# Reordering the start of an attention kernel by the parts of its loads, and moving one normalisation to DMA transposes

## The chip, the core and the metric

The kernel runs on one core of a Trainium2 chip. The metric is the device time of one execution in microseconds (us), quoted as the median of several runs. Every run quoted here is a fast one, so nothing below compares runs of different states. "Slot" and "iteration" are the kernel's own units: the attention part is a loop of 128 iterations (one key/value group and one tile of 128 query rows each), and every iteration has eight slots, each with one pair of score matmuls and one exponential over 128x1024 elements.

## The reference, cut to what matters

```python
mod = (_silu(c) @ w_mod).reshape(c.shape[0], 6, 1, -1)      # 512 -> 6 x 512
sa, ca, ga, sb, cb, gb = ...                                 # its six rows
h = _layernorm(x) * (1 + ca) + sa                            # x: 2048 x 512
x = x + ga * attention(h @ wq, k_cache, v_cache) @ wo        # 32 heads, 8 KV heads, Dh = 128
h = _layernorm(x) * (1 + cb) + sb
x = x + gb * mlp(h)                                          # gated MLP with a spatial mix
```

Before the first score can be computed, the first tile of x must be normalised, the modulation columns `ca` and `sa` must be computed from 1 MB of `w_mod`, the tile must be transposed and modulated, multiplied by 512 KB of `wq`, and the keys must be transposed. All of that happens once, in the first 12 us.

## The kernel before: the parts that the change touches

The loads at the start are all issued on the same queue, in this order:

```python
nc.sync.dma_start(out=x_sb[:, 0, :], in_=x_dram[:, 0, :])
nc.sync.dma_start(out=wmod_a[:], in_=wmod_dram[:, :, 0 : 2 * D])          # 1 MB, one load
k_nat = early.tile([P, SK], BF16, name="kT")
nc.sync.dma_start(out=k_nat[:, 0:HK].rearrange("p (t d) -> p t d", d=DH), in_=k_rows)
...
load_wq(0, nc.sync)                                                        # 512 KB
nc.sync.dma_start(out=x_sb[:, 1:CT, :], in_=x_dram[:, 1:CT, :])
```

The modulation is computed column by column, so that its first column already needs the whole of `wmod_a`. Then come the transposes of the first tile, the K transposes with one copy, and the projection:

```python
warm(14)                                     # zero matmuls that keep TensorE busy
xns0 = ln1_norm(0, 1, ln1_stats(0, 1))
mod_columns(0, wmod_a, 0)                    # for each of 8 columns: 4 matmuls, kt = 0..3
ln1_turn(0, 1, xns0, on_act=(1, 3))          # 2 x (2 transposes, 1 DVE and 1 ACT copy of one bank)
k_ps = bank("o_ps")[:].bitcast(BF16)
for kt in range(NKT // 2):                   # 8 transposes of K
    nc.tensor.transpose(k_ps[:, kt * P : (kt + 1) * P], k_nat[:, ...], ident[:])
nc.scalar.copy(out=kT0[:, 0:HK], in_=k_ps)
warm(1)
... qproj(0, list(range(REP)), 0, P, two_engines=True) ...   # 16 matmuls, DVE and ACT copy halves
warm(2)
first = dict(r1=ln1_stats(1, 1))             # statistics of tile 1 (the second tile)
ln_stats(mv1, 2, x_sb[:, 2, :])
first["x1"] = ln1_norm(1, 1, first["r1"])    # xn of the second tile
...
```

Chunk 1 (rows 512 to 1023) was normalised in iteration 1 and transposed by 16 TensorE transposes in its last slot, while chunks 2 and 3 already used DMA transposes:

```python
if ch == 1:
    at(*turn, lambda: ln1_turn(ch * CT, CT, st["x"]))
else:
    at(norm[0], norm[1] + 1, lambda: ln1_dma(ch * CT, CT, st["x"]))
    at(*turn, lambda: ln1_dma_mod(ch))

ln1_at(1, (1, 1), (1, 5), (1, 7))            # statistics, normalisation, transposes
```

## Time and profile before

| | before |
|---|---|
| time, median of 6 runs | 1326.84 us (1326.76 to 1327.12) |
| span of the profiled run | 1325.4 us |
| TensorE busy | 98% |
| ScalarE busy | 81% |
| VectorE busy | 36% |
| first scores start | 11.71 us |
| TensorE gap at chunk 1's transposes | scores reappear at 29.23 us, ScalarE idle 2.16 us |

The lines themselves stand in the prediction below. In a line of the timeline the columns are: start in us, length in us, engine, source line, operation, output<-input, shape, and how many instructions the line sums up. What stands in brackets at the end is the idle time of that engine before the line, and the instruction that ended it. Source lines differ between the kernels, because the change adds lines: the scores are L928 before and L980 after, the exponentials L935 and L987, the projection of the first tile L885 and L921, the copies of q L897/L899 and L929.

### The profile page before, as it was taken

To read this page: it belongs to the slowest core of one execution; us is meant where nothing else is said; L and a number is where in the kernel's file an instruction comes from. 1 tells how busy PE (TensorE), PEld (TensorE's weight loads), DVE (VectorE), ACT (ScalarE), POOL (GpSimd) and SP (SyncE) were. 2 spreads that over 40 slices of the span, in tenths; PEclk is the share of its full clock that TensorE was granted. 3 is DMA by queue.
4 is the path that set the end of the run, shared out by engine and by line. 5 is a ranking of instruction groups with operands and counts; after the bars stand their busy time and mean duration, and the time that the engine had idled before them with its cause. 6 is when DMAs were issued, how large, how long until landed. Compare 5 with 4: busy or idle time off the path is not lost.

```text
span 1325.4 us, 27685 instructions
## 1 busy us (share of the span) xinstructions
PE 1302.4 (98%) x12142; PEld 859.2 (65%) x12349; DVE 473.3 (36%) x1166; ACT 1078.4 (81%) x1061; POOL 49.0 (4%) x92
## 2 busy tenths in 40 slices
PE   8999999999999999999999999999999999999997
PEld 5666666666666666666666666666666666644444
DVE  5532222222222222222222222222222566793444
ACT  6898999999999999999999999999999999650000
POOL 1200000000000000000000000000000000120000
PEclk9999999999999999999999999999999999999999
DMA  5451021102111111111110211021101121143300
GB/s 162 111 134 30 16 49 37 37 13 53 23 31 33 34 37 37 29 37 37 33 33 17 53 37 31 19 52 25 30 13 21 25 34 33 29 115 82 66 21 27
DMA packets 145984, 57.59 MB, mean 43 GB/s; under 512 B 136160, under 2 KB 141408, under 8 KB 145856
## 3 DMA queue, kind: packets, MB, share of 16 engines
q1 hardware_dynamic: 139200, 37.32, 14.4%
q0 software_dynamic: 4208, 16.39, 4.4%
q10 hardware_dynamic: 2448, 2.03, 0.6%
q8 instruction: 98, 1.61, 0.5%
q14 instruction: 30, 0.25, 0.1%
HBM read 21.37 MB, written 2.10 MB: 18 GB/s over the span
## 4 chain that ended last, share of the span: by engine, by line
PE 97%; issue 1%; DVE 1%; DMA 0%; POOL 0%; ACT 0%; SPq 0%; DVEq 0%
PE s_ps L928 35%; PE o_ps L950 35%; PE misc L885 7%; PE misc L1290 7%; PE misc L982 6%; PE s_ps L1136 2%; PE s_ps L1175 2%; PE o_ps L1311 1%; DMA wmod_a<-in_w_mod_dram 0%; PE s_ps L1311 0%; DVE bnst L691 0%; PE misc L833 0%; DVE xn L680 0%; PE misc L782 0%; PE misc L1052 0%
## 5 line engine op out<-in xcount | busy, mean ns | idle before, releaser
L935 ACT ACTIVATE pT<-s_ps 128x1024 bf16<-128x1024 f32 x1024 | 1044.5, 1024 | 84.3 <-PE s_ps L928 10.1
L950 PEld LDWEIGHTS <-pT 128*128 128x128 bf16 x8192 | 548.5, 98 | 241.2
L950 PE MATMUL o_ps<-v,pT 128*128 128x129 bf16 x8192 | 631.4, 220 | 0.0
L928 PE MATMUL s_ps<-qT,kT 128*128 128x512 bf16 x2048 | 609.0, 379 | 10.3 <-ACT qT L899 0.5
L961 DVE RECIPROCAL rall<-o_ps 128x2 f32<-128x2 f32 x256 | 43.7, 171 | 743.6 <-PE o_ps L950 743.3
L928 PEld LDWEIGHTS <-kT 128*128 128x128 bf16 x2048 | 199.2, 98 | 119.5 <-issue 1.2
L885 PE MATMUL misc<-hT,wq_g 128*128 128x512 bf16 (+2 forms) x482 | 167.8, 365 | 0.3 <-ACT hT L842 0.2
L982 PE MATMUL misc<-wo_g,oT 128*128 128x512 bf16 x385 | 145.9, 379 | 0.0
L962 DVE TENSOR_TENSOR onorm<-o_ps,rall 128x256 bf16<-128x256 f32 x256 | 108.7, 425 | 8.8
L1290 PE MATMUL misc<-wsp,z 128*128 128x512 bf16 (+2 forms) x555 | 100.5, 336 | 0.6 <-issue 0.3
L897 DVE CAST qT<-misc 128x512 bf16<-128x512 f32 (+1 forms) x128 | 86.9, 679 | 7.6 <-PE misc L885 7.5
L1290 PEld LDWEIGHTS <-z 128*128 128x128 bf16 x560 | 50.6, 98 | 48.5
L995 DVE TENSOR_TENSOR xacc<-misc,xacc 128x512 f32<-128x512 f32 x112 | 76.2, 680 | 0.0
L885 PEld LDWEIGHTS <-wq_g 128*128 128x128 bf16 x544 | 51.5, 98 | 1.5 <-DMA wq_g<-in_A_wq_dram 0.3
L982 PEld LDWEIGHTS <-oT 128*128 128x128 bf16 x512 | 50.1, 98 | 0.7
L1305 DVE TENSOR_TENSOR gb<-misc,bsp_bc 128x512 bf16<-128x512 f32 (+1 forms) x28 | 18.4, 658 | 58.3 <-PE misc L1290 58.3
L1136 PE MATMUL s_ps<-win_sb,hT 128*128 128x448 bf16 x128 | 27.0, 352 | 0.1
L1146 ACT ACTIVATE z<-s_ps 128x896 bf16<-128x896 f32 x16 | 14.7, 917 | 14.9 <-PE s_ps L1136 14.9
L1175 PE MATMUL s_ps<-hT,win_sb 128*128 128x512 bf16 x109 | 24.3, 379 | 0.2
L1183 ACT ACTIVATE z1T<-s_ps 128x1024 bf16<-128x1024 f32 x14 | 14.3, 1024 | 10.1 <-PE s_ps L1175 9.1
L691 DVE BATCH_NORM_STATS2 bnst<-x_sb 128x6 f32<-128x512 bf16 x32 | 21.8, 682 | 0.5
L706 POOL DMA_DIRECT2D wq_g<-in_A_wq_dram x7 | 5.3, 753 | 420.9 <-PE misc L885 420.9
(79 smaller groups left out, 279.5 us busy)
## 6 DMA issues: line engine op xcount, KB each, us to landing
wq_g<-in_A_wq_dram POOLq DMA_DIRECT2D x7, 512.0 KB, 3.9
v<-in_A_v_cache_dram POOLq DMA_DIRECT2D x7, 512.0 KB, 6.6
wo_g<-in_A_wo_dram POOLq DMA_DIRECT2D x7, 512.0 KB, 4.7
oT<-onorm SPq DMA_TRANSPOSE x128, 2.4
wsp<-in_w_mod_dram POOLq DMA_DIRECT2D x1, 2048.0 KB, 9.1
out_dram<-yout ACTq DMA_DIRECT2D x15, 128.0 KB, 1.7
win_sb<-in_B_w_in_dram POOLq DMA_DIRECT2D x1, 1792.0 KB, 9.4
x_sb<-in_A_x_dram SPq DMA_DIRECT2D x3, 512.0 KB, 5.5
```

What stands on the lines that cost most here:

```text
L885: nc.tensor.matmul(ps[0][:, o0 : o0 + n], lhsT=wqs[g][:, dt, hh * DH : (hh + 1) * DH], rhs=hTs[ch][:, dt, c0 : c0 + n], start=(dt == 0), s ...
L897: nc.vector.tensor_copy(out=dst[:, 0:cut], in_=src[:, 0:cut])
L928: nc.tensor.matmul(s_ps[:, h * 512 : (h + 1) * 512].rearrange("p (r q) -> p r q", r=REP), lhsT=groups[g]["kT"][:, kt * P : (kt + 1) * P], ...
L935: nc.scalar.activation(out=pTs[u][:, 2 * i : 2 * i + 2, :], in_=s_ps[:].rearrange("p (k q) -> p k q", k=2), func=ACT.Exp, scale=inv_sqrt_dh,)
L950: nc.tensor.matmul(o_ps[:, hh % 2, 0 : DH + 1], lhsT=pTs[u][:, kt, hh * P : (hh + 1) * P], rhs=groups[g]["v1"][:, kt, 0 : DH + 1], start=( ...
L961: nc.vector.reciprocal(out=rall[:, c0 : c0 + 2], in_=o_ps[:, :, DH])
L962: nc.vector.tensor_tensor(out=onorms[u][:, hh - 1 : hh + 1, :], in0=o_ps[:, :, 0:DH], in1=rall[:, c0 : c0 + 2].unsqueeze(2).to_broadcast([ ...
L982: nc.tensor.matmul(X_ps[:], lhsT=oTs[u][:, hh, :], rhs=groups[g]["wo"][:, hh, :], start=(hh == 0), stop=(hh == REP - 1),)
L995: nc.vector.tensor_tensor(out=xaccs[j][:], in0=X_ps[:], in1=xaccs[j][:], op=ALU.add)
L1136: nc.tensor.matmul(ps[0][:, hf * 512 : hf * 512 + FC], lhsT=h2Ts[j // CT][:, dt, (j % CT) * P : (j % CT + 1) * P], rhs=win_sb[:, dt, FH + ...
L1175: nc.tensor.matmul(ps[0][:, k * 512 : (k + 1) * 512], lhsT=win_sb[:, dt, f * P : (f + 1) * P], rhs=h2Ts[2 * ch2 + k][:, dt, :], start=(dt ...
L1290: nc.tensor.matmul(g_ps[:, :n], lhsT=z2[:, st, f * P : (f + 1) * P], rhs=wsp[t][:, st, c0 : c0 + n], start=(st == 0), stop=(st == NT - 1 a ...
```

## The change

The intent is that work on the first tile starts when a part of a load is there, not the whole, and that DVE and ACT never copy out of the same PSUM bank. On top of this, chunk 1 takes the DMA path that chunks 2 and 3 already have. The parts are: (1) `wmod` in four loads and the modulation summed part by part; (2) half of K loaded behind `wq`; (3) the first tile's transposes on two banks, and its projection into a tile of two banks; (4) the second K half copied by DVE behind the first scores, ahead of the second tile's normalisation; (5) chunk 1 by DMA transposes, with its statistics two slots earlier and its projection four slots later.

```diff
-    nc.sync.dma_start(out=wmod_a[:], in_=wmod_dram[:, :, 0 : 2 * D])
+    for kt in range(NDT):
+        nc.sync.dma_start(out=wmod_a[:, kt, :], in_=wmod_dram[:, kt, 0 : 2 * D])
...  (k_nat is loaded in two halves; the second one behind wq)
     load_wq(0, nc.sync)
+    load_k_nat(1)
     nc.sync.dma_start(out=x_sb[:, 1:CT, :], in_=x_dram[:, 1:CT, :])
...
-    warm(14)
     xns0 = ln1_norm(0, 1, ln1_stats(0, 1))
-    mod_columns(0, wmod_a, 0)
-    ln1_turn(0, 1, xns0, on_act=(1, 3))
...
+    mc_ps = bank("misc")
+    warm(10)
+    for kt in range(NDT - 1):
+        mod_part(kt, mc_ps)            # 8 one-column matmuls on part kt
+        warm(2)
+    ...                                # 4 transposes of xn, two in each of two banks
+    mod_part(NDT - 1, mc_ps)
+    mod_copy(0, mc_ps)
+    ...                                # hT: DVE copies one bank, ACT the other
+    k_turn((0, 1, 2, 3), (nc.vector.tensor_copy, nc.scalar.copy))
+    qTs = {0: early.tile([P, REP, 512], BF16, name="qT")}
+    q_ps = bank2()                     # ONE tile of two banks
+    ...                                # 16 projection matmuls, heads 0-1 in bank 0, 2-3 in bank 1
+    for hf, copy in enumerate((nc.vector.tensor_copy, nc.scalar.copy)):
+        copy(
+            out=qTs[0][:, 2 * hf : 2 * hf + 2, 0:P],
+            in_=q_ps[:, hf * 512 : hf * 512 + 2 * P].rearrange("p (h q) -> p h q", h=2),
+        )
...
+    def first_norm():                  # placed behind the first scores
+        k_turn((4, 5, 6, 7), (nc.vector.tensor_copy,))
+        ln_stats(mv1, 2, x_sb[:, 2, :])
+        first["x1"] = ln1_norm(1, 1, first["r1"])
...
-    ln1_at(1, (1, 1), (1, 5), (1, 7))
+    ln1_at(1, (0, 7), (1, 2), (2, 2))
...
-                it, slot = 2 + (2 + k) // 16, (1 + k // 2) % 8
+                it, slot = 2 + (10 + k) // 16, (5 + k // 2) % 8
```

More of the change, by code (lines that the diff above doesn't have):

```diff
@@ L697, with load_k_nat @@
     nc.sync.dma_start(out=x_sb[:, 0, :], in_=x_dram[:, 0, :])
-    nc.sync.dma_start(out=wmod_a[:], in_=wmod_dram[:, :, 0 : 2 * D])
+    for kt in range(NDT):
+        nc.sync.dma_start(out=wmod_a[:, kt, :], in_=wmod_dram[:, kt, 0 : 2 * D])
     k_nat = early.tile([P, SK], BF16, name="kT")
-    nc.sync.dma_start(out=k_nat[:, 0:HK].rearrange("p (t d) -> p t d", d=DH), in_=k_rows)
-    groups, wqs, hTs, qTs = {}, {}, {}, {}
+    def load_k_nat(half):
+        t0, t1 = half * NKT // 4, (half + 1) * NKT // 4
+        nc.sync.dma_start(
+            out=k_nat[:, t0 * P : t1 * P].rearrange("p (t d) -> p t d", d=DH),
+            in_=k_rows[:, t0:t1, :],
+        )
+    load_k_nat(0)
+    groups, wqs, hTs = {}, {}, {}
     def load_wq(g, engine):
@@ L788, in mod_columns, with mod_copy @@
                     )
+        mod_copy(first, mc_ps)
+    def mod_copy(first, mc_ps):
         c0 = first * NDT
@@ L822, in ln1_mod, with ln1_turn @@
         )
-    def ln1_turn(j0, n, xns, on_act=()):
+    def ln1_turn(j0, n, xns):
         ch, c0 = j0 // CT, (j0 % CT) * P
@@ L840, in ln1_turn @@
                 dst, src = hT[:, dt, c0 : c0 + n * P], t_ps[:, k, 0 : n * P]
-                if dt in on_act:
-                    nc.scalar.activation(
-                        out=dst,
-                        in_=src,
-                        func=ACT.Identity,
-                        scale=modc[:, NDT + dt : NDT + dt + 1],
-                        bias=modc[:, dt : dt + 1],
-                    )
-                else:
-                    ln1_mod(dst, src, dt)
+                ln1_mod(dst, src, dt)
     def ln1_dma(j0, n, xns):
@@ L859, in ln1_dma_mod, with mod_part @@
             ln1_mod(hTs[ch][:, dt, :], hTs[ch][:, dt, :], dt)
-    warm(14)
-    xns0 = ln1_norm(0, 1, ln1_stats(0, 1))
-    mod_columns(0, wmod_a, 0)
-    ln1_turn(0, 1, xns0, on_act=(1, 3))
-    k_ps = bank("o_ps")[:].bitcast(BF16)
-    for kt in range(NKT // 2):
-        nc.tensor.transpose(
-            k_ps[:, kt * P : (kt + 1) * P], k_nat[:, kt * P : (kt + 1) * P], ident[:]
-        )
-    nc.scalar.copy(out=kT0[:, 0:HK], in_=k_ps)
+    def mod_part(kt, mc_ps):
+        for col in range(2 * NDT):
+            nc.tensor.matmul(
+                mc_ps[:, col : col + 1],
+                lhsT=wmod_a[:, kt, col * P : (col + 1) * P],
+                rhs=sc_bf[:, kt : kt + 1],
+                start=(kt == 0 and col == 0),
+                stop=(kt == NDT - 1 and col == 2 * NDT - 1),
+            )
@@ new lines, in k_turn @@
+    def k_turn(kts, copies):
+        n = len(kts) // len(copies)
+        for e, copy in enumerate(copies):
+            part = kts[e * n : (e + 1) * n]
+            k_ps = bank("o_ps")[:].bitcast(BF16)
+            for k, kt in enumerate(part):
+                nc.tensor.transpose(
+                    k_ps[:, k * P : (k + 1) * P], k_nat[:, kt * P : (kt + 1) * P], ident[:]
+                )
+            copy(out=kT0[:, part[0] * P : (part[-1] + 1) * P], in_=k_ps[:, 0 : n * P])
+    xns0 = ln1_norm(0, 1, ln1_stats(0, 1))
@@ new lines @@
+    mc_ps = bank("misc")
[3 more added lines that the diff above has]
+        warm(2)
+    x_ps = []
+    for half in range(2):
+        x_ps.append(bank(("misc", "o_ps")[half])[:].bitcast(BF16))
+        for k in range(2):
+            dt = 2 * half + k
+            nc.tensor.transpose(
+                x_ps[half][:, k * P : (k + 1) * P], xns0[0][:, dt * P : (dt + 1) * P], ident[:]
+            )
+    mod_part(NDT - 1, mc_ps)
+    mod_copy(0, mc_ps)
+    hT_of(0)
@@ new lines @@
+    for k in range(2):
+        ln1_mod(hTs[0][:, k, 0:P], x_ps[0][:, k * P : (k + 1) * P], k)
+        nc.scalar.activation(
+            out=hTs[0][:, 2 + k, 0:P],
+            in_=x_ps[1][:, k * P : (k + 1) * P],
+            func=ACT.Identity,
+            scale=modc[:, NDT + 2 + k : NDT + 3 + k],
+            bias=modc[:, 2 + k : 3 + k],
+        )
+    k_turn((0, 1, 2, 3), (nc.vector.tensor_copy, nc.scalar.copy))
+    qTs = {0: early.tile([P, REP, 512], BF16, name="qT")}
+    q_ps = bank2()
@@ new lines @@
+    for n, dt in enumerate((0, 2, 1, 3)):
+        for hh in range(REP):
+            c0 = hh // 2 * 512 + hh % 2 * P
+            nc.tensor.matmul(
+                q_ps[:, c0 : c0 + P],
+                lhsT=wqs[0][:, dt, hh * DH : (hh + 1) * DH],
+                rhs=hTs[0][:, dt, 0:P],
+                start=(n == 0 and hh % 2 == 0),
+                stop=(n == NDT - 1 and hh % 2 == 1),
+            )
+    for hf, copy in enumerate((nc.vector.tensor_copy, nc.scalar.copy)):
+        copy(
+            out=qTs[0][:, 2 * hf : 2 * hf + 2, 0:P],
+            in_=q_ps[:, hf * 512 : hf * 512 + 2 * P].rearrange("p (h q) -> p h q", h=2),
+        )
@@ L871, with qproj @@
     warm(1)
-    def qproj(b, heads, c0, n, two_engines=False):
+    def qproj(b, heads, c0, n):
         g, ch = divmod(b, NCH)
@@ L895, in mm @@
                 src = ps[0][:, 0 : len(hs) * n].rearrange("p (h q) -> p h q", q=n)
-                cut = len(hs) // 2 if two_engines else len(hs)
-                nc.vector.tensor_copy(out=dst[:, 0:cut], in_=src[:, 0:cut])
-                if two_engines:
-                    nc.scalar.copy(out=dst[:, cut:], in_=src[:, cut:])
+                nc.vector.tensor_copy(out=dst, in_=src)
         return [lambda hh=hh, dt=dt: mm(hh, dt) for hh in heads for dt in range(NDT)]
-    for fn in qproj(0, list(range(REP)), 0, P, two_engines=True):
-        fn()
-    warm(2)
     first = dict(r1=ln1_stats(1, 1))
-    ln_stats(mv1, 2, x_sb[:, 2, :])
-    first["x1"] = ln1_norm(1, 1, first["r1"])
-    ln_stats(mv1, 3, x_sb[:, 3, :])
-    first["r2"] = rstd_of(mv1[:, 2:4, :], 2, "ln1")
     NU = HKV * NT
@@ L1069 @@
     fill = {}
+    def first_norm():
+        k_turn((4, 5, 6, 7), (nc.vector.tensor_copy,))
+        ln_stats(mv1, 2, x_sb[:, 2, :])
+        first["x1"] = ln1_norm(1, 1, first["r1"])
+        ln_stats(mv1, 3, x_sb[:, 3, :])
+        first["r2"] = rstd_of(mv1[:, 2:4, :], 2, "ln1")
     def first_turn():
@@ L1075 @@
     at(0, 5, lambda: ln1_turn(2, 2, first["x2"]))
-    for i in (0, 1, 2, 4):
+    fill[0, 0] = [first_norm]
+    for i in (1, 2, 4):
         fill[0, i] = [lambda: warm(1)]
@@ L1085, in ln1_at @@
         at(*norm, lambda: st.update(x=ln1_norm(ch * CT, CT, st["r"])))
-        if ch == 1:
-            at(*turn, lambda: ln1_turn(ch * CT, CT, st["x"]))
-        else:
-            at(norm[0], norm[1] + 1, lambda: ln1_dma(ch * CT, CT, st["x"]))
-            at(*turn, lambda: ln1_dma_mod(ch))
-    ln1_at(1, (1, 1), (1, 5), (1, 7))
+        at(norm[0], norm[1] + 1, lambda: ln1_dma(ch * CT, CT, st["x"]))
+        at(*turn, lambda: ln1_dma_mod(ch))
+    ln1_at(1, (0, 7), (1, 2), (2, 2))
     ln1_at(2, (2, 4), (3, 1), (4, 5))
```

## The prediction

> **What bounds the kernel now.** I read the page of the profile first: busy time by engine and the chain that ended last.
>
> ```profile
> PE 1302.4 (98%) x12142; PEld 859.2 (65%) x12349; DVE 473.3 (36%) x1166; ACT 1078.4 (81%) x1061; POOL 49.0 (4%) x92
> ...
> PE 97%; issue 1%; DVE 1%; DMA 0%; POOL 0%; ACT 0%; SPq 0%; DVEq 0%
> ```
>
> TensorE is busy 98% of a span of 1325.4 us and makes up 97% of the chain. No later wait is long enough to swallow a saving, so whatever TensorE gains near the start should reach the end. All TensorE idleness together is 1325.4 - 1302.4 = 23 us, and warm-up matmuls count as busy, so this change of the first 50 us can win a few microseconds, never the 26.5 us that would be 2%.
>
> Then I read the timeline of the first 50 us. The start:
>
> ```profile
> 5.88 0.41 DVE L680 TENSOR_SCALAR xn<-x_sb,mv,rstd_ln 128x512 bf16<-128x512 bf16 x1 [1.02 <-POOL rstd_ln L676]
> ...
> 7.34 0.95 PE L782 MATMUL misc<-sc_bf,wmod_a 128*128 128x1 bf16 x32 [1.30 <-DMA wmod_a<-in_w_mod_dram]
> ...
> 8.41 0.15 DVE L791 TENSOR_SCALAR modc<-misc 128x4 f32<-128x4 f32 x1
> ...
> 9.05 0.81 ACT L842 ACTIVATE hT<-misc,modc 128x128 bf16<-128x128 bf16 x2 [5.82 <-DVE hT L815]
> ...
> 9.54 1.08 PEld L885 LDWEIGHTS <-wq_g 128*128 128x128 bf16 x16 [0.30 <-DMA wq_g<-in_A_wq_dram]
> ...
> 10.83 0.42 DVE L897 CAST qT<-misc 128x256 bf16<-128x256 f32 x1 [1.54 <-PE misc L885]
> ...
> 11.17 0.68 DVE L691 BATCH_NORM_STATS2 bnst<-x_sb 128x6 f32<-128x512 bf16 x1
> 11.29 0.37 ACT L899 CAST qT<-misc 128x256 bf16<-128x256 f32 x1 [0.53 <-DVE qT L897]
> 11.71 0.59 PE L928 MATMUL s_ps<-qT,kT 128*128 128x512 bf16 x2 [0.49 <-ACT qT L899]
> ```
>
> Two loads (wmod, then wq) and two serial pairs of copies decide when the first scores (L928) start, at 11.71. The second query tile then waits for its own normalisation; here are its xn, its transposes, and the scores behind them:
>
> ```profile
> 13.09 0.41 DVE L680 TENSOR_SCALAR xn<-x_sb,mv,rstd_ln 128x512 bf16<-128x512 bf16 x1 [0.22 <-POOL rstd_ln L676]
> ...
> 13.56 0.40 PE L833 MATMUL misc<-ident,xn 128*128 128x128 bf16 x4 [0.39 <-DVE xn L680]
> ...
> 13.79 0.59 PE L928 MATMUL s_ps<-qT,kT 128*128 128x512 bf16 x2
> ```
>
> And the one large hole afterwards, the normalisation of chunk 1:
>
> ```profile
> 26.36 0.61 PE L950 MATMUL o_ps<-v,pT 128*128 128x129 bf16 x8
> ...
> 27.53 1.87 PE L833 MATMUL misc<-ident,xn 128*128 128x128 bf16 x16 [0.56 <-DVE xn L680]
> ...
> 29.23 0.59 PE L928 MATMUL s_ps<-qT,kT 128*128 128x512 bf16 x2
> ...
> 29.86 2.89 ACT L935 ACTIVATE pT<-s_ps 128x1024 bf16<-128x1024 f32 x3 [2.16 <-PE s_ps L928]
> ```
>
> The in-order TensorE reaches 16 transposes whose input the DVE and GpSimd have not finished. The last of the eight o_ps matmuls has issued by 26.36 + 0.61 - 0.22 (one matmul's latency) + 0.06 = 26.80; the next scores start at 29.23. ScalarE starves for 2.16 us.
>
> [...] ACT's hT at 9.05 waits for DVE's hT, ACT's CAST of qT at 11.29 waits 0.53 us for DVE's CAST, both pairs from one bank. [...] So the single 1 MB wmod load releases nothing before its end (issue to landing 6.1 us here), and four loads give four release points. [...] (0.95 - 0.16)/31 = 25 ns for the one-column matmuls, 0.59 - 0.38 = 0.21 us for scores. [...] Here a 128x512 bf16 scaling from PSUM takes 0.54 us (0.45 apart), from SBUF 0.41 us (0.33 apart).
>
> **Part 1, wmod in four loads, modulation by part.** Same bytes, same 2 KB pieces, same queue: the last part should land where the whole did, about 7.3. Three quarters of the 32 one-column matmuls and the four transposes of xn (ready at 6.3) move ahead of that. After the landing there remain 8 matmuls: 24 x 25 ns = 0.6 us saved, so the modc copies start near 7.7 instead of 8.33. With x_ps on two banks, DVE does two hT copies and ACT two, side by side: about 8.1 to 8.7 and 8.1 to 8.9, where ACT ended at 9.86 before.
>
> **Part 2, half of K after wq.** hT is now ready before wq, so wq's landing binds: 2.57 + 6.9 = 9.47 before. 128 KB fewer are ahead of it; at the roughly 380 GB/s that the queue moved in that stretch this is 0.34 us, so about 9.15. I assume the extra issues on SP (about 0.4 us each) stay hidden behind the backlog of the queue.
>
> **Part 3, projection.** 16 matmuls x 56 ns + 0.22 = 1.1 us, so 10.3; the two qT copies now read two banks in parallel: 0.42 instead of 11.66 - 10.83 = 0.83. First scores at 10.3 + 0.42 + 0.05 = 10.8, that is 0.9 earlier.
>
> **Part 4, the second tile gives most of that back.** The second K half is copied by the DVE behind the first scores, in front of the second tile's xn. First statistics: x_sb tiles 1 to 3 land at 3.04 + 7.5 = 10.54, so 10.65. K copy after the K transposes: 10.8 + 0.43 (two scores issued) + 0.44 (four transposes with latency) = 11.65, for 0.5. Statistics of tile 2 from 12.1, aggregation 12.8, xn at 12.9 instead of 13.09. TensorE then idles between the second scores and the transposes, as before. So from the third slot on the shift is only 0.2 us.
>
> **Part 5, chunk 1 by DMA transposes.** Sixteen TensorE transposes (0.9 us) and the wait before them go. Scores could start at 26.80 instead of 29.23, a gain of 2.43. But ScalarE is the pacer just there: with two score buffers, scores of a slot wait for the exp two slots back. Its run of six from 22.10 lasts 5.60, to 27.70; so iteration 2 starts at 27.75 instead of 30.12: 2.36. The five slots of iteration 2 without projection then run at ScalarE's 0.905 instead of TensorE's 0.885: minus 0.1. What replaces it: statistics (4 x 0.79 on DVE) from about 18.3, xn by 24.4, four DMA transposes (1.2 us of SP each, 2.5 to land) by about 30, modulation about 31.4, first projection with it about 32.5. It should not wait. Moving the projection from slots 1 to 7 of iteration 2 into iterations 2 and 3 leaves its sum alone.
>
> **Sum.** 2.36 - 0.1 + 0.2 = about 2.5 us. 1326.8 - 2.5 = 1324.3 us.
>
> **The rivals.** (a) The new chunk 1 path is late: the DMA transposes land after 32.5, and TensorE waits at the first projection of chunk 1. For it: later ones of this kind took 3.6 to 14.7 us to land; against: those ran beside a 2 MB load, and at 25 to 30 us the queues are empty. It would cost 1 to 2 us: 1325.5. (b) SP becomes the limit at the start: eight issues before the x tiles instead of five; if they stall, wq and the x tiles land up to 1 us later and the K copy in front of xn makes the second tile later than before. For it: one earlier issue took 1.35 us, the transposing one 3.3 us. It would turn the +0.2 into -0.6: 1325.1. (c) The early start carries through, because the x tiles come sooner or the DVE order costs less: up to 0.9 more, 1323.5. (d) Nothing arrives, ScalarE taking over as bound: against it, ACT is at 81% and shows 0.2 to 0.3 us of idleness per slot with projection.
>
> **Range and chances.** Centre 1324.3; (a) and (b) set the upper edge at 1325.7, (c) the lower one at 1323.0. 2% either way lies ten times outside these terms: faster 0.005, within 2% 0.99, slower 0.005.
>
> **What would show it.** Right: first scores near 10.8, modc near 7.7, no L885 wait but for wq; xn of tile 2 near 12.9; no hole of TensorE near 27; iteration 2's first scores near 27.6; 17 TensorE matmuls fewer. Wrong: TensorE idle before the first projection of chunk 1 near 32 (rival a), wq landing at or after 9.5 (b), or ScalarE without gaps through iterations 2 and 3 (d).

In the paragraph ahead of Part 1 are readings of the trace of before. The 56 ns of Part 3 are in that trace, too: (0.61 - 0.22)/7 from its eight K transposes (L867, 0.61 us together, 219 ns for one). What rested on the cut passages was the author's estimate: that copies out of two banks run side by side, and that a load releases nothing before its end. For the second, the traces have this: with one load, landed at 7.30 (1.19 + 6.11), the first modulation matmul started at 7.34; with four, in the changed kernel, the parts ran at 4.94, 5.88, 6.52 and 7.39.

## The result and the profile after

The changed kernel takes 1325.82 us (median of 6 runs, 1325.43 to 1326.52) against 1326.84 us (6 runs, 1326.76 to 1327.12). Ratios here are the mean time of one kernel's fast runs over that of the other's fast runs of the same rounds, so they are not quite the ratio of the medians quoted: 0.9993, with a 95% interval of 0.998 to 1.0006. The interval includes 1, though the slowest run of the changed kernel (1326.52) is below the fastest of before (1326.76). That is "the same" at 2%, and a gain of 1.0 us in the medians. The prediction was 1324.3 with a range up to 1325.7: it claimed 2.5 us and 1.0 us came. Note also the spread: 1.1 us between the changed kernel's runs, 0.4 us before.

First the page of the changed kernel: busy time by engine, and the chain that ended last.

```profile
PE 1313.2 (99%) x12332; PEld 858.6 (65%) x12332; DVE 473.2 (36%) x1168; ACT 1077.8 (81%) x1061; POOL 49.4 (4%) x92
...
PE 98%; DMA 0%; DVE 0%; SPq 0%; issue 0%; ACT 0%
```

The bound has not changed. The TensorE figures of the two pages can't be compared by themselves, because the trace of before lacks about 200 matmul records (12142, against 12349 weight loads). The weight loads can: 12349 before, 12332 now, 17 fewer, as predicted.

Next the timeline of the start of the changed kernel, in the order of the prediction's steps.

```profile
7.77 0.16 DVE L803 COPY modc<-misc 128x4 f32<-128x4 f32 x1 [1.48 <-PE misc L868]
...
8.10 0.81 ACT L908 ACTIVATE hT<-o_ps,modc 128x128 bf16<-128x128 bf16 x2 [4.87 <-DVE modc L804]
...
9.63 0.90 PEld L921 LDWEIGHTS <-wq_g 128*128 128x128 bf16 x16 [0.57 <-DMA wq_g<-in_A_wq_dram]
...
10.74 0.42 DVE L929 CAST qT<-s_ps 128x256 bf16<-128x256 f32 x1 [1.91 <-PE s_ps L921]
...
11.20 0.37 ACT L929 CAST qT<-s_ps 128x256 bf16<-128x256 f32 x1 [1.56 <-DVE qT L929]
11.62 1.01 PE L980 MATMUL s_ps<-qT,kT 128*128 128x512 bf16 x2 [0.70 <-ACT qT L929]
...
13.09 0.42 DVE L886 COPY kT<-o_ps 128x512 bf16<-128x512 bf16 x1 [1.11 <-PE o_ps L883]
13.44 0.69 DVE L691 BATCH_NORM_STATS2 bnst<-x_sb 128x6 f32<-128x512 bf16 x1
...
14.25 0.38 DVE L680 TENSOR_SCALAR xn<-x_sb,mv,rstd_ln 128x512 bf16<-128x512 bf16 x1
```

Three things are to be seen. The modulation and hT come when they were expected (7.77 and 8.10), in this profile; the experiments show (end of e11) that this was the earliest of six. TensorE then waits for `wq` until 9.63, later than before (9.54). And ACT's copy of q at 11.20 still waits for DVE's copy. So the first scores start at 11.62, only 0.09 us earlier than before. Everything behind them is later: xn of the second tile comes at 14.25, where it was 13.09.

Part of this lateness has a cause that the prediction did not name. The first scores took 1.01 us where a pair took 0.59 before. The view by stretches of time gives, for each stretch, its length, then busy time and instructions of PE, PEld, DVE, ACT and POOL, then the granted TensorE clock, DMA share and GB/s. The stretch from 11 to 14 us of the changed kernel:

```profile
11.00:14.00 3.00, 2.38 (x9) 0.97 (x8) 1.85 (x5) 1.45 (x3) 0.81 (x2) 0.55 1.31 246
```

The granted clock is 0.55 there. The clock records of the trace put the half clock at 11.27 to 14.68 us, 3.41 us long. No such stretch is in the profile of before at this place.

The second half of the story is chunk 1. The view by stretches for 26 to 31 us, before and then after:

```profile
26.00:31.00 5.00, 4.17 (x48) 2.88 (x46) 3.44 (x11) 2.84 (x4) 1.02 (x1) 1.00 0.02 5
```

```profile
26.00:31.00 5.00, 5.00 (x58) 3.69 (x56) 0.86 (x3) 5.00 (x7) 0.00 (x0) 1.00 0.65 107
```

The hole is gone: TensorE and ScalarE are busy for all of the 5 us, where ScalarE was busy for 2.84. The timeline shows that nothing takes its place when the transposed chunk is first used:

```profile
23.23 12.02 ACT L987 ACTIVATE pT<-s_ps 128x1024 bf16<-128x1024 f32 x13 [0.41 <-PE s_ps L980]
...
24.79 5.18 SPq L859 DMA_TRANSPOSE hT<-xn  x4
...
32.49 1.38 DVE L828 TENSOR_SCALAR hT<-hT,modc 128x512 bf16<-128x512 bf16 x4 [2.81 <-DMA hT<-xn]
...
34.35 0.59 PE L947 MATMUL misc<-hT,wq_g 128*128 128x512 bf16 x2
```

Thirteen exponentials run without a gap from 23.23 to 35.25. The DMA transposes landed about 2.4 us later than the prediction's "about 30", yet the modulation is over at 33.87 and the projection follows at 34.35 directly behind other TensorE work.

To see where time comes and goes, compare the start of every exponential with the same one before. Minus is earlier than before:

```
                       iteration,slot   0,0    0,1    0,2    1,6    1,7    2,5    from 3,5 on
changed, profiled run                  +0.32  +0.68  +1.13  +1.13  -1.19  -2.79   -1.07
```

The start loses 1.13 us, chunk 1 gains 2.32 us (from +1.13 to -1.19), and moving the projection from iteration 2 into iteration 3 gives and takes back the same amount but 0.12. From there the shift is constant until the end of attention.

### The profile page after: what moved, and what is told of

Its sections match the earlier page's. It is cut to its first block, busy times and chain, and to the rows that moved or that the text cites. A ratio compares the mean times of both kernels' runs of the same rounds, so it can differ in the third digit from the quotient of the medians.

```text
span 1324.6 us, 27877 instructions
## 1 busy us (share of the span) xinstructions
PE 1313.2 (99%) x12332; PEld 858.6 (65%) x12332; DVE 473.2 (36%) x1168; ACT 1077.8 (81%) x1061; POOL 49.4 (4%) x92
## 4 chain that ended last, share of the span: by engine, by line
PE 98%; DMA 0%; DVE 0%; SPq 0%; issue 0%; ACT 0%
PE o_ps L1002 35%; PE s_ps L980 33%; PE misc L1034 8%; PE misc L947 8%; PE misc L1347 7%; PE s_ps L1193 2%; PE s_ps L1232 2%; PE o_ps L1368 1%; PE s_ps L1368 1%; DMA wq_g<-in_A_wq_dram 0%; PE misc L1104 0%; SPq L699 0%; PE misc L1355 0%; PE s_ps L921 0%; PE misc L846 0%; DVE yout L1384 0%
## 5 line engine op out<-in xcount | busy, mean ns | idle before, releaser
L1034 PE MATMUL misc<-wo_g,oT 128*128 128x512 bf16 x512 | 194.0, 379 | 0.0
L947 PE MATMUL misc<-hT,wq_g 128*128 128x512 bf16 (+2 forms) x528 | 189.6, 371 | 0.0
L958 DVE CAST qT<-misc 128x512 bf16<-128x512 f32 x127 | 86.3, 680 | 2.0 <-PE misc L947 1.9
```

The costliest lines, as they stand in the source:

```text
L947: nc.tensor.matmul(ps[0][:, o0 : o0 + n], lhsT=wqs[g][:, dt, hh * DH : (hh + 1) * DH], rhs=hTs[ch][:, dt, c0 : c0 + n], start=(dt == 0), s ...
L958: nc.vector.tensor_copy(out=dst, in_=src)
L1034: nc.tensor.matmul(X_ps[:], lhsT=oTs[u][:, hh, :], rhs=groups[g]["wo"][:, hh, :], start=(hh == 0), stop=(hh == REP - 1),)
```

## The experiments

All twelve gave correct results, and all are "the same" at the 2% level; what is read here are tenths. The sets ran on different chips (e1 to e4 on one, e0 and e5 to e7 on a second, e8 to e10 on a third, e11 on a fourth). The 95% interval of the ratio leaves out 1 for e1 (0.9965 to 0.9998), e10 (0.9966 to 0.9999) and e5 (1.0003 to 1.0036) alone; e8's ends at 1.0000. The other differences lie within intervals about 2 us wide on either side, so they are differences of medians, to be read together with the traces.

| run | median us (runs) | before, same rounds | difference | ratio |
|---|---|---|---|---|
| e1_chunk1_only | 1324.81 (4) | 1327.05 (7) | -2.24 | 0.9982 |
| e2_start_only | 1328.02 (4) | 1327.05 | +0.97 | 1.0006 |
| e3_warm_wait | 1325.84 (4) | 1327.05 | -1.21 | 0.999 |
| e4_split_q | 1325.34 (4) | 1327.05 | -1.71 | 0.9986 |
| e0_after_again | 1325.64 (4) | 1326.98 (7) | -1.34 | 0.999 |
| e5_one_wmod | 1329.46 (4) | 1326.98 | +2.48 | 1.0019 |
| e6_kcopy_late | 1325.77 (4) | 1326.98 | -1.21 | 0.9991 |
| e7_repaired | 1327.99 (4) | 1326.98 | +1.01 | 1.0006 |
| e8_start_mended | 1325.02 (4) | 1327.20 (7) | -2.18 | 0.9983 |
| e9_tile1_early | 1325.57 (4) | 1327.20 | -1.63 | 0.9985 |
| e10_chunk1_again | 1325.05 (4) | 1327.20 | -2.15 | 0.9982 |
| e11_four_loads | 1327.50 (4) | 1327.03 (7) | +0.47 | 1.0005 |

### Chunk 1 alone (e1), and the start alone (e2)

The kernel before with nothing but the new path for chunk 1, and the changed kernel with the old path.

```diff
 # e1: edits in the kernel before; e2 undoes the same lines in the changed one
-        if ch == 1:
-            at(*turn, lambda: ln1_turn(ch * CT, CT, st["x"]))
-        else:
-            at(norm[0], norm[1] + 1, lambda: ln1_dma(ch * CT, CT, st["x"]))
-            at(*turn, lambda: ln1_dma_mod(ch))
+        at(norm[0], norm[1] + 1, lambda: ln1_dma(ch * CT, CT, st["x"]))
+        at(*turn, lambda: ln1_dma_mod(ch))
-    ln1_at(1, (1, 1), (1, 5), (1, 7))
+    ln1_at(1, (0, 7), (1, 2), (2, 2))
-                it, slot = 2 + (2 + k) // 16, (1 + k // 2) % 8
+                it, slot = 2 + (10 + k) // 16, (5 + k // 2) % 8
```

> The kernel before with only the new path of chunk 1 (statistics, DMA transposes, shifted projection), the start as before. Theory (the chunk 1 part is worth the 2.3 us that the two traces show between the exp of iteration 1 slot 6 and slot 7 and up to iteration 5, and the new start gives over 1 us of it back): 1324.4 to 1324.8, so faster than the changed kernel, with no half-speed stretch. Rival A (the chunk 1 part pays only together with the new start, or the last 0.2 of it is lost on the way): 1325.5 to 1326. In the trace the first scores should stand at 11.7 as before and the hole of TensorE near 27 be gone.

> The changed kernel with the path of chunk 1 as before, so the new start alone. Theory: slower than the kernel before, by 1.1 us in runs in which the TensorE clock is halved near 11 to 15 us (mean clock 0.996 or 0.997), by about 0.5 in the others: 1327.2 to 1328.0. Rival A (the start is neutral): 1326.8. The prediction on record would have said 1326.6.

Chunk 1 alone took 1324.81 us, 2.24 us less than before, and is faster than the whole change. The start alone took 1328.02 us, 0.97 us more than before. The two add up to -1.27; the whole change measured -1.02 and -1.34 when repeated (e0, below). So the halves add up within the scatter, and the start is the half that costs time. The trace of e2, at full clock all through its start, says the same: its exponentials are 0.23 us late at slot 0,0 and 0.84 us late from slot 0,2 on. In the trace of e1 the exponentials are 0.21 us early already at the start, where its code equals that of before: `wmod` happened to land at 7.13 instead of 7.34. So 0.2 us is the scatter that a single profile of the start has, and 2.54 - 0.21 = 2.33 us at slot 1,7 and 2.41 - 0.21 = 2.20 us at the end are the worth of chunk 1.

### The changed kernel once more (e0)

No edit; the same kernel on another chip, to see what a second profile says of the half clock.

> The changed kernel itself once more, as the reference for the others of this job on the same chip. Expected 1.0 us below the kernel before, as on record, with a spread of up to 1 us and a mean clock of 0.996 or 0.997 in the slower runs. Its last wmod part should land between 7.3 and 8.4 us, and wq between 9.5 and 10.2.

It took 1325.64 us. Its profile has full clock in the stretch from 11 to 14 us (view by stretches; the seventh figure behind the length is the clock):

```profile
11.00:14.00 3.00, 1.46 (x9) 0.61 (x8) 2.44 (x8) 2.19 (x3) 0.81 (x2) 1.00 1.31 243
```

and its timeline, with the K copy and the second tile's xn:

```profile
11.56 0.59 PE L980 MATMUL s_ps<-qT,kT 128*128 128x512 bf16 x2 [0.70 <-ACT qT L929]
...
12.41 0.42 DVE L886 COPY kT<-o_ps 128x512 bf16<-128x512 bf16 x1 [0.49 <-PE o_ps L883]
...
13.57 0.38 DVE L680 TENSOR_SCALAR xn<-x_sb,mv,rstd_ln 128x512 bf16<-128x512 bf16 x1
```

The first scores are at nearly the same place as in the profile on record (11.56 against 11.62), but the K copy comes at 12.41 instead of 13.09 and xn at 13.57 instead of 14.25. So the half clock costs 0.68 us where it falls. Without it the exponentials stand at -0.16, -0.16 and then +0.45 from slot 0,2 on: the second tile's xn, 0.48 us later than before (13.09), costs 0.61 us between the second slot and the third. The kernel before has no K copy there.

What does the half clock cost in the time? Every run has its mean clock. In the first set of six, the two runs with 0.996 and 0.997 took 1326.34 (the profiled one) and 1326.52 us, the other four, with 0.998 or 0.999, took 1325.43 to 1325.83. That is 0.8 us for a run in which the half clock falls, and, as an estimate, 0.3 us in the mean of that set. All four of e0's runs have 0.998 or 0.999. So the half clock goes with the spread. It doesn't explain the missing gain: the runs at full clock are still only 1.2 us below the kernel before, where chunk 1 alone is 2.2. The kernel before has such runs too, but seldom: two of the 28 with a clock (1328.08 and 1328.48 us, both 0.997).

For the projection's wait the timeline of e0 has these two lines:

```profile
9.24 0.27 PE L883 MATMUL o_ps<-ident,kT 128*128 128x128 bf16 x2 [1.09 <-ACT hT L908]
...
9.57 0.90 PEld L921 LDWEIGHTS <-wq_g 128*128 128x128 bf16 x16 [0.23 <-DMA wq_g<-in_A_wq_dram]
```

Here TensorE waited only 0.23 us for `wq`: until then it was held by ACT's hT and the K transposes behind it, because the last part of `wmod` came late in this run (the modulation copy is at 8.05 instead of 7.77).

Of these two profiles of one kernel, then, one has the 3.41 us long stretch of half clock and the other has not. In the three microseconds ahead of it (8 to 11 us) TensorE was busy 1.55 us in the run with half clock and 1.70 us in the run without, against 2.58 us in the kernel before: the change thins TensorE's work out just there. No gap of TensorE between 5 and 11.3 us was longer than 1.03 us (7.93 to 8.96) in the run with half clock.

That the thinner work brings the half clock is the author's reading; it is not shown, and the views by stretches give no limit. From 8 to 11 us TensorE was busy 1.75 us in e6, whose mean clock from 11 to 14 us was 0.60, and 1.68 us in e4, whose clock was 1.00 there. In the six profiles with 2.23 to 2.90 us (e8 2.23, e11 2.38, the kernel before 2.58, e1 2.59, e10 2.60, e3 2.90) it was 1.00 as well. And e0 itself had only 1.46 us from 11 to 14 us, and a clock of 1.00 from 14 to 17 us.

### More zero matmuls while wq is awaited (e3)

```diff
+    w_ps = bank2()
+    for k in range(5):
+        nc.tensor.matmul(w_ps[:, 0:512]..., lhsT=zeros[:, 0, :], rhs=zeros[:], start=True, stop=True)
     k_turn((0, 1, 2, 3), (nc.vector.tensor_copy, nc.scalar.copy))
```

> The changed kernel plus five 512-column matmuls on zeros into a score bank, placed where TensorE waits for ScalarE and for wq. Theory (the half clock [...] costs because the K transposes and scores of slots 0 and 1 stand before the DVE's K copy and so before the second tile's xn): no run has a clock below 0.998, xn of the second tile near 13.7 instead of 14.25, worst runs 0.5 us faster than those of the changed kernel, median 1325.3 to 1325.6. Rival B (the half clock costs nothing, TensorE waits there anyway): median unchanged at 1325.8 with the same spread of 1.1 us.

It took 1325.84 us (1325.64 to 1326.15), 1.21 us less than before, no better than the changed kernel itself (1.34 less, on another chip). Its profile had full clock and first scores at 11.69. TensorE was busy 2.90 of 3 us from 8 to 11 us, so the edit does what it was made for, and none of the four runs shows a half clock (0.998 to 0.999). But none of e0's four does either, and the time does not show the expected gain: the median is above the expected 1325.3 to 1325.6. From 11 to 14 us it was busy only 1.46 us, as in e0, so this edit moves the thin stretch more than it removes it. The run is inconclusive on what the half clock costs on average.

### The two halves of q in two tiles (e4)

```diff
-    q_ps = bank2()
+    q_ps = [bank2(), bank2()]
...
-                q_ps[:, c0 : c0 + P],
+                q_ps[hh // 2][:, c0 : c0 + P],
...
-            in_=q_ps[:, hf * 512 : hf * 512 + 2 * P].rearrange("p (h q) -> p h q", h=2),
+            in_=q_ps[hf][:, 0 : 2 * P].rearrange("p (h q) -> p h q", h=2),
```

> The changed kernel with the first projection in two tiles of one bank each instead of one tile of two banks; the built order shows that ScalarE's copy of qT then waits for TensorE alone. Theory: the two copies run side by side, first scores about 0.4 us earlier (11.2 instead of 11.6), xn of the second tile up to 0.4 earlier where the DVE's K copy binds, so 0.2 to 0.4 us off the total: 1325.4 to 1325.6. Rival (the second tile's statistics bind, not the scores): unchanged, 1325.8.

The timeline of e4 shows the two copies of q:

```profile
11.20 0.42 DVE L929 CAST qT<-s_ps 128x256 bf16<-128x256 f32 x1 [1.37 <-PE s_ps L921]
11.31 0.37 ACT L929 CAST qT<-s_ps 128x256 bf16<-128x256 f32 x1 [0.67 <-PE s_ps L921]
```

They start 0.11 us apart and both wait for TensorE; in the changed kernel they started 0.46 us apart and ACT waited for DVE. So the serialisation came from the two banks belonging to one tile, not from the banks themselves. The time is 1325.34 us, 1.71 us less than before, which is 0.37 us better than e0's gain; the gap of the copies that vanished is 0.46 - 0.11 = 0.35 us. That the two agree is no proof: e0 ran on another chip in other rounds, and 0.37 us is within the scatter. The order of the copies is shown, its worth in the time is not. In this profile `wmod`'s last part and `wq` were both late (projection at 10.21), so the first scores stand at 11.74 all the same: single profiles of this start can't be compared to a tenth.

### wmod in one load again (e5), and the repair built on it (e7)

```diff
-    for kt in range(NDT):
-        nc.sync.dma_start(out=wmod_a[:, kt, :], in_=wmod_dram[:, kt, 0 : 2 * D])
+    nc.sync.dma_start(out=wmod_a[:], in_=wmod_dram[:, :, 0 : 2 * D])
```

> The changed kernel with wmod in one load again (everything else as changed). Theory C (the four loads finish later than the one: with the split the queue moves 150 to 350 GB/s between 4 and 7 us instead of 380, so the last part lands at 7.3 to 8.4 instead of 7.1 to 7.3, and wq at 9.5 to 10.2 instead of 9.3 to 9.5): last wmod landing at 7.3 or earlier, modc at 7.9 or 8.3, wq at 9.2 or earlier, first scores near 11.2 to 11.3, total 0.3 to 0.6 us below the changed kernel of the same rounds. Rival (the scatter of the landings has to do with the run, not with the split): wmod landing scatters as before and the total is the same as the changed kernel's within 0.1.

This was a miss: it took 1329.46 us, 2.48 us more than before. The loads did what was expected. `wmod` was there at 7.04 and `wq` landed at 9.27 (issued at 2.57, 6.7 us to landing). But the zero matmuls that fill the waits between the four parts now stand behind the landing: the parts ran at 7.04, 7.68, 8.32 and 9.76. TensorE had also had nothing to do from 5.4 to 7.0, and its clock fell to half from 8.43 to 15.26 us (0.86 in the mean from 7 to 9 us, 0.50 from 9 to 15):

```profile
9.00:12.00 3.00, 2.01 (x23) 1.57 (x22) 1.02 (x5) 1.01 (x3) 0.00 (x0) 0.50 1.29 226
```

The projection took 1.91 us instead of 1.07, and the first scores came at 14.38. Work that was placed to fill a wait becomes a cost when the wait is taken away and the work is not. How much of the 2.48 us is this and how much the half clock isn't separated: the two slowest runs (1329.64 and 1329.82) have a mean clock of 0.999, the two others (1328.77 and 1329.29) 0.996 and 0.994. So here the mean clock does not go with the time; why was not looked at.

```diff
 # e7: e5 + the two q tiles of e4 + the K copy behind xn (e6, below)
```

> The three repairs together on the changed kernel: one wmod load, the projection in two tiles, the K copy behind xn of tile 2. Theory: the start is then as early as the kernel before's or earlier, so the total is that of chunk 1's path alone or up to 0.4 less: 2.2 to 2.6 us below the kernel before, 1324.4 to 1324.8. Rival (something else in the new start, such as K in two loads, costs): it stays 0.5 us or more above the run with chunk 1's path alone, 1325.3 or more.

It took 1327.99 us (1326.43 to 1328.64), 1.01 us more than before: a miss again, with half clock from 8.98 to 15.81 us (the projection took 1.91 us again) and the first scores at 13.88. Its fastest run (1326.43) is the only one with a mean clock of 0.998; the others have 0.994 to 0.996, so here the half clock goes with the loss.

### The K copy behind the second tile's xn (e6)

```diff
     def first_norm():
-        k_turn((4, 5, 6, 7), (nc.vector.tensor_copy,))
         ln_stats(mv1, 2, x_sb[:, 2, :])
         first["x1"] = ln1_norm(1, 1, first["r1"])
+        k_turn((4, 5, 6, 7), (nc.vector.tensor_copy,))
```

> The changed kernel with the DVE's copy of the second K half placed behind the second tile's statistics and xn instead of in front. Theory D (the K copy in front of the statistics of tile 2 is what moves slot 2 and everything after it by 0.6 us against slots 0 and 1): the jump of 0.6 us between the exp of slot 1 and of slot 2 against the kernel before falls to 0.2 or less, total 0.4 to 0.6 us below the changed kernel of the same rounds, near 1325.3. Rival (the late first scores bind, through the serial copies and wq): total unchanged within 0.1.

It took 1325.77 us, 1.21 us less than before, not better than e0 (1325.64). Its profile fell on a half-clock run (0.60 in the mean from 11 to 14 us): first scores at 11.63, and xn at 13.01 instead of 14.25. So the copy's place does decide when xn comes. But the transposes behind xn ran only at 14.14, at the low clock and behind the K transposes, and the shift at the end of attention was -1.52, 0.45 us better than the profile on record (-1.07). One sign is clear: in the four profiles of this start at full clock (e0, e2, e3, e4) the shift jumps by 0.6 us between slots 0,1 and 0,2. In e6 it is +0.70 in slot 0,1 and +0.68 from slot 0,4 on; with the copy behind xn the jump is gone. But two of the four runs had a half clock (0.997), and the median does not show the gain, so the worth of the copy's place in total is not settled.

### The start mended throughout (e8), with chunk 1 alone beside it (e10)

```diff
 # e8: the changed kernel with e5, e4 and e6, and
-    warm(10)
-    for kt in range(NDT - 1):
-        mod_part(kt, mc_ps)
-        warm(2)
+    warm(14)
...                          # transposes of xn stay here
-    mod_part(NDT - 1, mc_ps)
+    for kt in range(NDT):
+        mod_part(kt, mc_ps)
...
+    w_ps = bank2()           # 3 zero matmuls behind the modulation
```

> The changed kernel with the new start mended in five places: one wmod load, its 32 matmuls in one go after it and all warm-up matmuls (14) before it, three more on zeros into a score bank while wq is awaited, the projection in two tiles, the DVE's K copy behind xn of tile 2. Theory (the loss of the new start is the sum of the split load, the warm-ups between its parts, the serial qT copies and the K copy): wmod lands at 7.0 to 7.3, modc near 8.1, wq at 9.1 to 9.3, first scores at 10.8 to 11.0, xn of tile 2 near 12.7, no half clock, total 0.2 to 0.5 us below the run with chunk 1's path alone of the same rounds, about 1324.4. Rival (the half clock comes back whatever the order, or K in two loads costs): equal to the run with chunk 1's path alone or slower.

> The kernel with chunk 1's path alone once more, on the same chip and in the same rounds as the two others: 2.2 us below the kernel before.

Now the first scores start where the prediction wanted them. The timeline of e8:

```profile
10.96 0.59 PE L986 MATMUL s_ps<-qT,kT 128*128 128x512 bf16 x2 [0.24 <-ACT qT L935]
...
13.02 0.41 DVE L885 COPY kT<-o_ps 128x512 bf16<-128x512 bf16 x1
13.16 0.40 PE L845 MATMUL misc<-ident,xn 128*128 128x128 bf16 x4 [0.73 <-DVE xn L680]
...
14.17 1.07 DVE L827 TENSOR_SCALAR hT<-misc,modc 128x128 bf16<-128x128 bf16 x4
...
16.64 4.98 ACT L993 ACTIVATE pT<-s_ps 128x1024 bf16<-128x1024 f32 x5 [0.57 <-PE s_ps L986]
```

The first two exponentials are 0.75 us earlier than before. The third waits for the second tile's transposes, which are only 0.40 us earlier (13.16 against 13.56), and is 0.29 us earlier. The fifth, at 16.64 against 16.71, is 0.07 us earlier, and so are all that follow until chunk 1. DVE takes the rest: xn of the second tile is 0.40 us earlier (12.69 against 13.09), but the K copy behind it takes 0.41 us, so the modulation of the second tile starts at 14.17 where the kernel before had 14.24:

```profile
14.24 1.07 DVE L815 TENSOR_SCALAR hT<-misc,modc 128x128 bf16<-128x128 bf16 x4
```

The time is 1325.02 us, 2.18 us less than before; chunk 1 alone in the same rounds took 1325.05 us, 2.15 less. A start with these faults mended is worth 0.03 us, less than the scatter. Five edits were made together here, and none of them is priced alone.

### The second tile's x loaded with the first (e9)

```diff
-    nc.sync.dma_start(out=x_sb[:, 0, :], in_=x_dram[:, 0, :])
+    nc.sync.dma_start(out=x_sb[:, 0:2, :], in_=x_dram[:, 0:2, :])
...
+    first["x1"] = ln1_norm(1, 1, ln1_stats(1, 1))     # right behind the first tile's
```

> The same with the second tile of x loaded together with the first, so that the DVE makes its statistics and xn while wmod is awaited, and the statistics of tiles 3 and 4 right behind the qT copy. Theory (from slot 2 on only the second tile's xn binds, not the scores of slots 0 and 1): wmod and wq land about 0.3 us later, first scores near 11.2, but no wait between slots 1 and 2, exp of slot 2 near 13.6 instead of 14.4, and all after it 0.8 to 1.2 us earlier than in the run with chunk 1's path alone: about 1323.8. Rival (the later landing of wmod and wq takes the gain away): not below the run with chunk 1's path alone.

The four runs were 1326.58, 1324.56, 1327.04 and 1324.49 us. The two good ones are about 0.5 us below chunk 1 alone (1325.05), which fits the reading that the second tile binds; the two bad ones are 1.5 to 2 us above it. The profile fell on a bad one: `wmod` landed at 9.1 us (issued at 1.24, 7.9 us to landing, where e8 had 5.9) and the clock was half from 9.41 to 12.82 us (0.57 in the mean from 9 to 12, 0.86 from 12 to 15). Both bad runs have a mean clock of 0.997, both good ones 0.998 or 0.999. Why it landed so late was not found, and whether it did so in the other bad run is not known.

### Four loads of wmod and nothing else (e11)

```diff
 # the kernel before with
-    nc.sync.dma_start(out=wmod_a[:], in_=wmod_dram[:, :, 0 : 2 * D])
+    for kt in range(NDT):
+        nc.sync.dma_start(out=wmod_a[:, kt, :], in_=wmod_dram[:, kt, 0 : 2 * D])
```

> The kernel before with wmod in four loads and nothing else. Theory C (the split itself delays the landings): last wmod part at 7.3 to 8.3 us instead of 7.1 to 7.3, wq at 9.6 to 10.3 instead of 9.3 to 9.5, so the first scores 0.2 to 0.8 us later and, as everything hangs on the projection here, the total 0.2 to 0.8 us above the kernel before of the same rounds. Rival (the late landings in the changed kernel come from the other order of the loads, such as half of K behind wq): landings and total as before, within 0.1.

It took 1327.50 us, 0.47 us more than before in the medians. That is not clear of the noise (interval of the ratio 0.9988 to 1.0022): three of its four runs lie at 1327.47 to 1327.51, and the runs of before reach 1327.51. The timeline of e11 shows the projection's weight loads waiting 0.76 us for `wq`, until 9.91, where the kernel before had 9.54:

```profile
9.91 0.89 PEld L886 LDWEIGHTS <-wq_g 128*128 128x128 bf16 x16 [0.76 <-DMA wq_g<-in_A_wq_dram]
```

The first scores come at 11.90 instead of 11.71, and the exponentials are 0.18 to 0.19 us late. Two things differ ahead of this wait, and neither is shown to be its cause. The timeline of the issuing queue gives the issue of `wq`, in the kernel before and in the changed one:

```profile
2.57 0.43 SPq L706 DMA_DIRECT2D wq_g<-in_A_wq_dram  x1
```

```profile
1.20 1.85 SPq L699 DMA_DIRECT2D wmod_a<-in_w_mod_dram  x4
3.09 0.43 SPq L704 DMA_DIRECT2D kT<-in_A_k_cache_dram  x1
3.56 0.43 SPq L715 DMA_DIRECT2D wq_g<-in_A_wq_dram  x1
```

Four issues take 1.85 us where one took 0.69, so `wq` is issued 0.99 us later. And the transfer rate of the first 15 us, in 40 slices of 0.375 us each, is this before and then in e11:

```profile
GB/s 0 0 0 0 3 150 200 93 66 71 257 317 371 388 393 350 393 404 382 382 385 382 374 358 344 312 201 139 285 288 255 223 244 215 236 238 325 350 341 352
```

```profile
GB/s 0 0 0 0 3 130 323 246 295 251 279 257 306 371 317 279 320 292 259 284 360 358 374 385 363 316 182 88 98 282 289 226 225 244 218 228 240 238 352 363
```

With four loads the queues start their bulk earlier (slices 7 to 10), but between about 5.2 and 7.5 us they move 260 to 320 GB/s instead of 350 to 400. The two cancel: summed over the slices, both rows have moved about 1.58 MB by 7.5 us and 2.39 MB by 9.75 us. So in this pair a slower queue is not why `wq` lands later; which of its parts came last these views do not show. What goes with four loads of 256 KB here is a later landing of what lies behind them. Over the profiles, `wq` landed (its issue plus its time to landing) as follows:

```
wmod in one load,   all of K first (before, e1, e10):       9.47  9.27  9.56               mean 9.43
wmod in one load,   half of K behind wq (e5, e7, e8):       9.27  9.07  8.97               mean 9.10
wmod in four loads, all of K first (e11):                   9.85
wmod in four loads, half of K behind wq
                    (record, e0, e2, e3, e4, e6):           9.56  9.56  9.86  9.66  10.16  9.57   mean 9.73
```

Only e9's bad run (10.82) is left out, with its other load of x and its late `wmod`. Half of K behind `wq` brings it 0.33 us forward (9.43 to 9.10); the split puts it back by 0.42 us (9.43 to 9.85) or 0.63 us (9.10 to 9.73).

The same profiles say what the split brought its own consumer. The first copy of the modulation columns (modc) starts at:

```
wmod in one load, all 32 matmuls behind it (before, e1, e10, e8):  8.33  8.12  8.38  8.15               mean 8.25
wmod in four loads, all 32 behind them (e11):                      8.24
wmod in four loads, summed by part (record, e0, e2, e3, e4, e6):   7.77  8.05  8.68  8.40  8.77  8.10   mean 8.30
```

So the 0.6 us that the split was to bring are there in the profile on record alone, the earliest of six. In the other five the last parts landed later, at 7.42 to 8.33 us, where the single load landed at 7.00 to 7.34.

## Why the prediction was wrong, step by step

**Part 1, wmod in four loads: failed at "the last part should land where the whole did, about 7.3".** In the profile on record the modulation came at 7.77 (predicted near 7.7) and hT at 8.10 to 8.91 (predicted 8.1 to 8.9), side by side on DVE and ACT. That was luck: over the six profiles with this start the modulation came at 8.30 in the mean, and with one load at 8.25. The sum (24 matmuls at 25 ns) was right, and the later landing ate it. The sentence "Same bytes, same 2 KB pieces, same queue" took the split as free, for its own last part and for what comes behind it.

**Part 2 failed at "I assume the extra issues on SP (about 0.4 us each) stay hidden behind the backlog of the queue".** `wq` was to land at 9.15 and landed at 9.56. The 0.34 us for the half of K was right (0.33 us in the means above). But with the split of Part 1 `wq` is issued 0.99 us later and lands 0.4 to 0.6 us later in the means: more than the half of K brings. e11, which has the split and nothing else, shows this in its trace (9.85 against 9.47); its time is 0.47 us longer, within the noise. Whether the later issue makes the later landing or something else in the queue does is not shown.

**Part 3, "the two qT copies now read two banks in parallel", failed.** They read two banks, but of one tile, and the program as built orders the two engines by tile. ACT waited for DVE as before. e4, with two tiles, removes the wait: its copies started 0.11 us apart (11.20 and 11.31) instead of 0.46 us (10.74 and 11.20). The first scores came at 11.56 (e0) instead of 10.8: 0.42 us from the later start of the projection (9.57 against 9.15) and some 0.35 us from the copies. In e0 only 0.23 us of this start was a wait for `wq` itself, the rest was the late last part of `wmod`; in the profile on record the wait for `wq` was 0.57 us.

**Part 4 was right in its mechanism and started from a wrong time.** The prediction had xn of the second tile 2.1 us behind the first scores (10.8 to 12.9); it came 2.01 us behind them in e0 (11.56 to 13.57). Because the first scores had not moved, the K copy in front of xn now lay open: a gain of 0.2 us became a loss of 0.45 us. The caveat that this part "gives most of that back" was right to the full in e8: with first scores at 10.96, only 0.07 us are left after five slots.

**Part 5 was right.** It claimed 2.36 us less 0.1. The trace gives 2.32 us at slot 1,7 of the changed kernel (2.33 in e1) and 0.12 us of it is lost in iterations 2 and 3; alone it measured 2.24 and 2.15 us. The first projection did not wait, though the DMA transposes landed late, so rival (a) and rival (d) fall.

**The sum and the rivals.** The wrong term of the sum is "+ 0.2" for the start, which measured -0.97 us (e2). Rival (b), the loads as the limit at the start with wq after 9.5 and the K copy making the second tile late, is what happened, and its test ("wq landing at or after 9.5") fired. But the test is a weak one: in e10, whose start is that of before, `wq` landed at 9.56 too. That issuing on SP is the limit, as (b) has it, is not shown. Its size, -0.6 us, is about that of the traces with full clock (-0.45 in e0, -0.84 in e2). What it lacked is the half clock, which nothing in the prediction names: in some runs it takes 0.7 to 0.8 us more and makes the changed kernel's runs scatter over 1.1 us. It is not what the gain failed on: e2's loss of 0.97 us was measured in four runs at full clock. Rival (c), the early start carrying through, is refuted by e8. Two slips of the reading, without consequence: the issues ahead of the x tiles went from four to eight, not from five to eight, and the "23 us" of TensorE idleness counts the 207 matmuls that the trace of before lacks as idle time (the page after shows 1324.6 - 1313.2 = 11.4 us).

**What stays open.** Why `wq`, and the last part of `wmod`, land later with four loads; how much of the losses of e5 and e7 is the half clock and how much the misplaced zero matmuls; what the K copy's place is worth in total (e6); why `wmod` landed at 9.1 us in e9; and what makes the clock fall in one run and not in another.

The best version that runs in all runs alike is the kernel before with chunk 1's new path alone: 1324.81 and 1325.05 us in two sets, 2.2 us below before and about 1 us below the whole change.

## What to carry to other kernels

When a change has several parts, price each on the path and then measure each alone: here one part was worth all of the gain and more, and the other part cost 1 us of it. Before a step of the start is shortened, look for the next thing that the same slots wait for; the first scores came 0.75 us earlier in e8 and the fifth slot did not notice, because the second tile's normalisation on DVE set its time. Splitting a load to let its consumer start early brought that consumer forward in one profile of six here, and the load behind it landed later in the mean; so look at the landings in several profiles before the gain is counted. Zero matmuls that fill a wait have to be moved when the wait is moved, and a change that thins TensorE's work near the start should be checked for the granted clock in several profiles; here it was 0.55 from 11 to 14 us in one profile of the changed kernel and 1.00 in another.
